# Diagonal sums of five chunks on four 64x64 tiles of TensorE, three unread wide products ahead of it, and every order written anew

## The chip, the cores and the metric

One core of one Trainium2 chip runs the whole program in one launch. The metric is the device time of one execution in microseconds (us); of the kernel before, three executions are shown, and a fourth was profiled.

## What is computed

Four sequences of 768 tokens pass through a recurrent attention with 8 heads of 48 features, and then through a gated network:

```python
for t in range(S):                                   # per batch b and head h
    cur = u * k[t] (outer) v[t]
    y[t] = r[t] @ (state + cur)
    state = w[:, None] * state + k[t] (outer) v[t]   # w, u: one number per head and feature
h = relu(y @ w_in)                                   # 384 -> 1024, halves u and v of 512
v_n = (v - mean) / sqrt(var + 1e-6)                  # over the 512 features
v_s = w_spatial @ v_n + b_spatial                    # over the 768 tokens of the sequence
out = (u * v_s) @ w_out                              # 512 -> 384
```

All of it is float32, and the weights come in float64 halves and other raw forms that the kernel converts itself.

## The kernel before

A sequence is cut into 6 chunks of 128 tokens, so there are 24 chunks, numbered m. The recurrence inside a chunk becomes products: heads are taken in pairs p = 0..3, and a chunk in two halves of 64 tokens, so that a pair's two heads and a chunk's two halves fill the four 64x64 corners of TensorE. For each chunk

- `load` brings r and k with features on partitions (tile rk), and r, k, v with tokens on partitions (rkv);
- `prep` scales rk by powers of the decay (tile tt, a table made at the start from wt: a scan and a reciprocal on VectorE, L346 and L351, then one copy on ScalarE), turns k over on TensorE for the first three chunks ("kt", L434) and makes the diagonal term;
- `scores` makes the products of k and r ("sc", L486) and of k and v ("st", L498) in 64-wide corners;
- `mid` masks the scores into tile a (L509) and moves the state on (sbb L514 or L516, ps L520, sba L526 or L529);
- `xsum` adds state times r ("rs") and scores times v ("av", both L537) in the one accumulator xp;
- `xout` folds xp together (ScalarE copy cp L582, TensorE "xa" L587) and splits the result in a high and a low part xh and xl (L600, TensorE "xl" L604, L606).

xp is a single buffer, so the rs of a chunk begins only when the copies of the chunk before have read it.

The diagonal term is a sum over 48 features of r, k, and a column of weights wu = w times u. For the first five chunks (ND_PE) TensorE makes it ("ds", L450): the product of r and k stands in tile a with two heads on the 128 partitions, and one matmul per pair with a moving operand of two columns (one per head, zero on the other head's partitions) gives two sums per token. For later chunks VectorE reduces instead. The sums go to tile dg, and from there `dia` (L470 on GpSimd, or eight small ScalarE operations) writes them on the diagonal of a.

The network's weights are split in two fp32r parts at the start: w_in in six blocks ("conv": four VectorE steps L634, L636, L639, L646, a ScalarE cast, and three matmuls 128x512 L654 to L656 on TensorE), w_spatial and w_out in a similar way. Every big product is then three fp32r matmuls (`mm3`, L738 to L740): V (nine matmuls 128x512 for a chunk), U, the spatial products, and the output.

The order is not found at run time. A planner in the file (class `Plan`) gave every operation a start, an engine and a buffer; the numbers are kept in the table SCHEDULE, and `plan.replay` reads them. Operations are issued in the order of their starts, so each engine and SyncE's queue of DMA transfers has a fixed order, and only semaphores decide when each begins. The buffers of the w_in conversions and of many products are the four PSUM tiles pm.

Of the kernel before, what the change touches and what calls it, by code (L numbers as in the profile page):

```python
# [11 lines left out]
ALU = mybir.AluOpType  # L12
# [6 lines left out]
P = 128  # L19
# [258 lines left out]
def fused_kernel(ctx, tc, rkT, rkvN, wT, uB, w_in, w_sp, b_sp, w_out, out):  # L278
# [4 lines left out]
    PAD0, PAD1 = 0, 32  # L283
# [38 lines left out]
    def dma(fn, nbytes, r=(), w=(), bufs=()):  # L322
        return op(SPQ, fn, r, w, bufs, nbytes)
# [11 lines left out]
    dma(lambda: nc.sync.dma_start(out=wt, in_=wT), 6144, w=["wt"])  # L335
# [9 lines left out]
    for p in range(NP):  # L345
# [9 lines left out]
    op(("POOL", 0.21, True), lambda: g.tensor_tensor(  # L355
        out=wu.rearrange("s (p j) -> s p j", j=2), in0=wt[:, 0:NP].unsqueeze(2).to_broadcast([P, NP, 2]),
        in1=wt[:, NP:3 * NP].rearrange("s (p j) -> s p j", j=2), op=ALU.mult), r=["wt"], w=["wu"])
# [14 lines left out]
    head = []  # L372
    tp = buf("pm")
# [30 lines left out]
    def prep(m):  # L404
# [24 lines left out]
        else:  # L429
# [5 lines left out]
            t["kt"] = op(("PE", 0.86, False), f, r=[(m, "k"), "eye"], w=[(m, "kt")], bufs=[rk, kp])  # L435
# [3 lines left out]
        if m < ND_PE:  # L439
            at = 448 + H * (m % 2)  # L440
# [13 lines left out]
            o.fn = lambda o=o: (s.copy if o.eng == "ACT" else lambda x, y: v.tensor_copy(out=x, in_=y))(  # L454
                dgs[dg.place].rearrange("s j p -> s p j"), ps[:, 0, at:at + H].rearrange("s (p j) -> s p j", j=2))
# [653 lines left out]
    "00000000h0dr10t08c09307l09u0ar0av0al07l0860b90qv0dc0rr1130qb0fw0qp0zn1431ac08r0c30a000b01902i0500b908r03r069"  # L1109
    "07i0ve0dn1by1870a00z50xw0u516y15r17o19l1gd1dn1ip1n00v50x20yz18713u1a51eq0jk0lh0ne0ol0pb10c1bq1bq1p11sh28x2h1"  # L1110
    "2kr3452372542d72772kv2wc30z1ue2f42iy2l02ms2qj2vd33u0fq0hn0ht0n90jq0u50wf0xw0mp0p011x0r90u61050sg14s0na0s90vv"
    "0yt0uc0y919x1ai16y1dw1ir1fv1o11wb17i18n1de1fb1i31tv2252qo3b41mg1oi11r1gu1gb1vr1ix1qc1x321b21o20929b2282b82c8"
    "1qw1s21uf1zl20t25s2it2q42x123q2d81nn1m41qy1xq2bu2op2tr2fu2hj2xu2p52q52r52ge2im2mr2pv2r832l3in3m73rv3xl3yn43l"
    "48r4au4bd4oj4ky4eo1oi1r02ua30f24827e2xg2fu2oh3ap3ba3a238n3gc3am3bl3fd33538139d3bf3f23kn41u47a47u25s2fu3gr3it"
    "2jf2s835h37n3iv3nk3sq3x43vp41b3xo3l73md3nq3v13w93yh4534cs4if2wc3kn44j46l3lo3ze41545o4454d24fs48f4a44pa4g64lp"
    "4mp4ad4bw4dc4fv4h34kv4r54vo4yl51v53253l54454n55657s5a15ca1pr2hf2mz4bd4lb28a2sk2wa3p25u00wn1ku1ux1jg1s33533y5"
    "4sv3qg4em2713dn4nq2tz2zv19g2op32e2ao2pt36c3zj4b74n73qp53r3cf3hb4gj56f7a07ul4ql52f6nu6ux6wu71q4tc4wy5ej5h24w8"
    "4zl5gw5je59m5qu5x35z862865950m5m65sg62t75v7d85dy6ba6qr6ve73276q55a5v666s6ci6e86ji7ec7yc8598dt8zg9ha7mk7r89ps"
    "9roa61a9q6fm6si78a7ya8do8fc62a66y9b19np9t79ur1ap3p34rb4uf5vj6gi6s974a4t55935qx5yn6l26sa6w97gt2iy3713dt3s4478"
    "48x6tl7at2k731f33y3i93v93wz7k87rd96y9lb9mt8r88xk92588q8f28jnavrb5admkb1vbsvemcaenavwaxe3it32l4xp4ys4ib3f24ow"  # L1120
    "3pp49a4br4ux4wm5cm5bn5jq5nq5165295535a346l48f5ia5kc55p4ve5oh5fj5zm66e60x5zi6fm6hj6ii6jo5mq5nw5r46375nf50m6jy"
    "6m06yh5d361o6a36e277w72l7167es73575o79t6oe6pk6qx6tu6p35m67io7kq7nz68x6wx6do7447cr7wz7vk8aw7zu86t8ct7vx7x47yg"
    "89c5oo6nu8ei8gk81v71h84v7hz87t8q68jt8ie8uy8kd8iy8qk8rw8tf8kw7mk8x08z296g7zg8t38ml8wv9du9e59cq9lh9iu9wba3s97v"
# [91 lines left out]
```

## Time and profile before

| | |
|---|---|
| three executions | 342.02, 343.79, 345.06 us (median 343.79) |
| profiled execution | 345.35 us, of which 343.2 us are the span from first to last instruction |
| TensorE busy | 329.7 us, 96% of the span |
| VectorE, ScalarE, GpSimd busy | 235.5, 169.5, 142.2 us |
| mean granted TensorE clock | 0.994 |

A row of the time line gives start, duration, engine, line, operation, and in brackets the idle time of the engine before it and what ended that. Matmuls overlap, so a row's duration holds some of the next; the chain of waits gives the part by which each piece moved the end on. "x8" counts instructions: a float32 matmul is two, a turn-over (transpose) is one.

### The profile page before, as it was taken

What the parts mean: (1) busy time and instruction counts of PE and PEld (TensorE: products, weight loads), DVE (VectorE), ACT (ScalarE), POOL (GpSimd) and SP (SyncE); (2) the same over time, 40 slices, a digit from 0 to 9 for tenths busy, and PEclk for the clock granted to TensorE, in tenths of its full rate; (3) what the DMA queues carried; (4) which work ended last, traced back from release to release, by engine and by line L of the source; (5) the groups of instructions that cost most, each with busy time, mean ns of one, the idle gap of its engine ahead of it and who ended that gap; (6) DMA issues with size and microseconds to landing.
All of it is one profiled execution on the core that took longest, in us unless ns stands there. A gap on an engine that the chain in (4) does not pass through costs nothing.

```text
span 343.2 us, 13056 instructions
## 1 busy us (share of the span) xinstructions
PE 329.7 (96%) x5832; PEld 301.0 (88%) x5832; DVE 235.5 (69%) x430; ACT 169.5 (49%) x428; POOL 142.2 (41%) x125
## 2 busy tenths in 40 slices
PE   3898999999999999999999999999999999999995
PEld 2767768899999888999999999999999999999995
DVE  6683887987969977769966858477865932726440
ACT  2252456885154365676544626673233776622231
POOL 3637358725829825383834122220944010125100
PEclk9998999999999999999999999999999999999999
DMA  7966676442341558322430440554200001100012
GB/s 233 356 217 238 233 224 247 155 178 97 127 138 43 187 165 270 136 77 85 138 136 5 156 159 3 159 161 150 78 4 2 4 0 70 48 1 2 1 68 92
DMA packets 14455, 41.53 MB, mean 121 GB/s; under 512 B 1728, under 2 KB 5312, under 8 KB 14400
## 3 DMA queue, kind: packets, MB, share of 16 engines
q1 hardware_dynamic: 14400, 40.71, 34.6%
q8 instruction: 45, 0.74, 0.9%
q14 instruction: 10, 0.08, 0.1%
HBM read 35.99 MB, written 4.72 MB: 119 GB/s over the span
## 4 chain that ended last, share of the span: by engine, by line
PE 92%; DVE 3%; DMA 2%; ACT 1%; issue 1%; SPq 0%; ACTq 0%
PE pm L738 25%; PE pm L740 23%; PE pm L739 23%; PE xp L537 9%; PE ps L486 4%; PE ps L498 3%; PE ps L450 2%; DMA raw<-w_in 2%; PE pm L654 1%; PE xp L587 1%; PE pm L434 0%; DVE hb L636 0%; DVE B L700 0%; DVE a L509 0%; DVE pm L634 0%
## 5 line engine op out<-in xcount | busy, mean ns | idle before, releaser
L738 PE MATMUL pm<-B,vh 128*128 128x384 f32 x102 | 34.9, 342 | 0.0
L834 POOL TENSOR_TENSOR g<-g,slot 128x384 f32<-128x384 f32 x14 | 16.2, 1160 | 43.6 <-DVE g L829 37.2
L740 PE MATMUL pm<-B,vl 128*128 128x384 f32 x102 | 34.2, 335 | 0.0
L739 PE MATMUL pm<-B,vh 128*128 128x384 f32 x102 | 34.1, 335 | 0.0
L738 PE MATMUL pm<-xh,wi_h 128*128 128x384 f32 x96 | 32.9, 342 | 0.0
L738 PE MATMUL pm<-wo_h,gt 128*128 128x384 f32 x96 | 32.6, 339 | 0.0
L739 PE MATMUL pm<-wo_l,gt 128*128 128x384 f32 x96 | 32.1, 335 | 0.3 <-issue 0.3
L740 PE MATMUL pm<-xh,wi_l 128*128 128x384 f32 x96 | 32.2, 336 | 0.0
L740 PE MATMUL pm<-wo_h,gt 128*128 128x384 f32 x96 | 32.2, 336 | 0.0
L739 PE MATMUL pm<-xl,wi_h 128*128 128x384 f32 x96 | 32.2, 335 | 0.0
L738 PE MATMUL pm<-wi_h,xh 128*128 128x512 f32 x72 | 29.8, 414 | 0.0
L740 PE MATMUL pm<-wi_h,xl 128*128 128x512 f32 x72 | 28.9, 401 | 0.0
L739 PE MATMUL pm<-wi_l,xh 128*128 128x512 f32 x72 | 28.8, 400 | 0.0
L836 DVE TENSOR_TENSOR gt<-g,gt 128x384 fp32r<-128x384 f32 x32 | 19.7, 622 | 13.1 <-ACT gt L835 13.1
L470 POOL TENSOR_TENSOR a<-diag,dg 128x512 f32<-128x512 f32 x20 | 23.2, 1162 | 13.3 <-ACT dg L454 7.6
L812 ACT ACTIVATE slot<-pm 128x384 f32<-128x384 f32 x32 | 15.6, 493 | 23.8 <-PE pm L740 23.8
L835 ACT CAST gt<-g 128x384 fp32r<-128x384 f32 x32 | 16.1, 508 | 19.1 <-POOL g L834 8.4
L738 PE MATMUL pm<-T,vh 128*128 128x384 f32 x72 | 24.4, 339 | 0.0
L582 ACT COPY cp<-xp 128x256 f32<-128x256 f32 (+1 forms) x24 | 8.5, 353 | 32.1 <-PE xp L537 27.0
L766 ACT ACTIVATE vs<-pm 128x512 f32<-128x512 f32 x24 | 14.4, 600 | 20.1 <-PE pm L740 20.1
L848 POOL TENSOR_TENSOR vl<-vs,vh 128x768 fp32r<-128x768 f32 x6 | 12.2, 2027 | 29.1 <-ACT vh L846 19.2
L740 PE MATMUL pm<-T,vl 128*128 128x384 f32 x72 | 24.1, 335 | 0.0
(148 smaller groups left out, 927.5 us busy)
## 6 DMA issues: line engine op xcount, KB each, us to landing
rkv<-rkvN SPq DMA_DIRECT2D x19, 608.0 KB, 4.9
rk<-rkT SPq DMA_DIRECT2D x21, 512.0 KB, 4.9
slot<-w_sp SPq DMA_DIRECT2D x12, 384.0 KB, 5.8
out<-ob SPq DMA_DIRECT2D x24, 192.0 KB, 2.4
raw<-w_in SPq DMA_DIRECT2D x6, 512.0 KB, 7.4
rk<-rkT SPq DMA_DIRECT2D x6, 256.0 KB, 5.4
rawo<-w_out SPq DMA_DIRECT2D x4, 384.0 KB, 5.9
rkv<-rkvN SPq DMA_DIRECT2D x2, 416.0 KB, 4.0
```

The lines of the kernel that those rows point to most:

```text
L470: g.tensor_tensor(out=A, in0=diag.unsqueeze(1).to_broadcast([P, H, HC]), in1=G.unsqueeze(2).to_broadcast([P, H, HC]), op=ALU.mult)
L486: te.matmul(ps[s0:s0 + 64, j, p * HC:(p + 1) * HC], R[hd, 1, p, s0:s0 + 64], R[hd, 0, p, t0:t0 + 64], start=True, stop=True, skip_group_ch ...
L537: te.matmul(xp[32 * p:32 * p + 32, bank, BASE[bank, z] + jt * HC:BASE[bank, z] + (jt + 1) * HC], lhsT, rhs, start=(bank, p) not in began, ...
L738: te.matmul(o, lh, rh, start=first, stop=False, skip_group_check=skip)
L739: te.matmul(o, lh, rl, start=False, stop=False, skip_group_check=skip)
L740: te.matmul(o, ll, rh, start=False, stop=last, skip_group_check=skip)
L766: op(("ACT", 0.79, False), lambda: s.activation(out=V, in_=pms[pm.place], func=AF.Relu, accum_out=su), r=[(b, "vp", c)], w=K + [("mv", n, ...
L812: op(act(TH, True), lambda: s.activation(out=slot(ub_, d % 2), in_=pms[pm.place][:, 0:TH], func=AF.Relu, scale=2.0), r=[(b, "up", t, d)], ...
L834: o.fn = lambda o=o: pick(o.eng).tensor_tensor(out=slot(gb), in0=slot(gb), in1=slot(ub_, d % 2), op=ALU.mult)
L835: op(act(TH), lambda: s.copy(slot(gt, 0), slot(gb)), r=[k], w=[(b, "gh", t, d)], bufs=[gt, gb], near=near)
L836: op(dve(TH, True), lambda: v.tensor_tensor(out=slot(gt, 1), in0=slot(gb), in1=slot(gt, 0).bitcast(F32), op=ALU.subtract), r=[k, (b, "gh", ...
L848: o.fn = lambda o=o: pick(o.eng).tensor_tensor(out=lv(), in0=src(), in1=hv().bitcast(F32), op=ALU.subtract)
```

## The change

- The ds of the first five chunks is cut into corners: 16 matmuls per chunk, each 64 partitions by 64 tokens with a moving operand of one column, in place of 4 of 128 by 128 with two columns. wu has one column per pair in place of two, wt shrinks from 12 to 8 columns, and the sums lie in both banks of ps.
- Three float32 matmuls of the identity with itself, 512 columns wide, are written into three pm tiles ahead of the first real TensorE work. Nobody reads them. They need only the tile eye (the identity, made on GpSimd).
- SCHEDULE is replaced whole: starts, engines and buffers of all operations. `pad0` changes from 0 to 8, a tile that nothing reads.

```diff
-    wt, w128, wu = T("wt", [3 * NP]), T("w128", [NP]), T("wu", [2 * NP])
+    wt, w128, wu = T("wt", [2 * NP]), T("w128", [NP]), T("wu", [NP])
...
+    def warm(b):
+        te.matmul(pms[b.place], eye, eye.unsqueeze(1).to_broadcast([P, 4, P]), start=True, stop=True)
+    for n in range(3):
+        wb = buf("pm")
+        head.append(op(("PE", 0.92, False), lambda wb=wb: warm(wb), r=["eye"], w=[("warm", n)], bufs=[wb]))
...
-            t["kt"] = op(("PE", 0.86, False), f, r=[(m, "k"), "eye"], w=[(m, "kt")], bufs=[rk, kp])
+            t["kt"] = op(("PE", 0.60, False), f, r=[(m, "k"), "eye"], w=[(m, "kt")], bufs=[rk, kp])
...
-            at = 448 + H * (m % 2)
+            at = 448 + NP * (m % 2)
...
-                    te.matmul(ps[:, 0, at + 2 * p:at + 2 * p + 2], PR()[:, p], wu[:, 2 * p:2 * p + 2],
-                              start=True, stop=True, skip_group_check=True)
-            t["ds"] = op(("PE", 0.50, False), f2, r=[(m, "a"), "wu"], w=[("psD", m % 2)], bufs=[a])
+                    for j in range(2):
+                        for z, s0, t0 in SUBS:
+                            hd = slice(64 * j, 64 * j + 64)
+                            te.matmul(ps[s0:s0 + 64, j, at + p:at + p + 1], PR()[hd, p, s0 // 64], wu[hd, p:p + 1],
+                                      start=True, stop=True, skip_group_check=True)
+            t["ds"] = op(("PE", 0.45, False), f2, r=[(m, "a"), "wu"], w=[("psD", m % 2)], bufs=[a], tiled=True)
...
 SCHEDULE = (
-    "00000000h0dr10t08c09307l09u0ar0av0al07l0860b90qv0dc0rr1130qb0fw0qp0zn1431ac08r0c30a000b01902i0500b908r03r069"
+    "02i00000h02x2950df0e60ex0fo0gl0gf0xr0df0370510u700005v0v30hp0b50fk0610lg0m50mu0x115m01o00f03s00b00005007i08r"
...
```

What the table does to the order is shown at three places; the numbers behind a tile's name tell its buffers apart, and new lines stand 4 to 7 further down in the file. The first is TensorE's beginning. Before:

```order
L375 MATMUL pm_115<-eye,tt 128x128
L434 MATMUL pm_116<-eye,rk_99 128x128 x4
L486 MATMUL ps<-rk_99 64x64 x16
L498 MATMUL ps<-rkv_102 48x48 x16
L375 MATMUL pm_115<-eye,tt 128x128
L537 MATMUL xp<-rk_99,sbb 32x64 x16
L450 MATMUL ps<-wu,a_94 128x2 x4
L434 MATMUL pm_116<-eye,rk_100 128x128 x4
L450 MATMUL ps<-wu,a_95 128x2 x4
L375 MATMUL pm_115<-eye,tt 128x128
L654 MATMUL pm_117<-hb,eye 128x512
L655 MATMUL pm_117<-lw,neg 128x512
```

With the change:

```order
L373 MATMUL pm_115<-eye 128x512
L373 MATMUL pm_116<-eye 128x512
L373 MATMUL pm_117<-eye 128x512
L379 MATMUL pm_118<-eye,tt 128x128 x3
L438 MATMUL pm_115<-eye,rk_99 128x128 x4
L493 MATMUL ps<-rk_99 64x64 x16
L505 MATMUL ps<-rkv_102 48x48 x16
L438 MATMUL pm_117<-eye,rk_100 128x128 x4
L457 MATMUL ps<-wu,a_94 64x1 x16
L544 MATMUL xp<-rk_99,sbb 32x64 x16
L379 MATMUL pm_118<-eye,tt 128x128
L661 MATMUL pm_116<-hb,eye 128x512
```

The second ds (of chunk 1) has moved from before the first w_in conversion to behind the second one, and behind the third conversion come now the scores and the k-v products of chunk 2 ahead of the first V; before, these two stood behind it.

The second place is SyncE's queue at the start. Before:

```order
L335 DMA wt<-wT 128x12
L395 DMA rk_99<-rkT 128x512 x2
L619 DMA raw<-w_in 128x1024
L401 DMA rkv_102<-rkvN 128x448
L395 DMA rk_100<-rkT 128x512 x2
L619 DMA raw<-w_in 128x1024
```

With the change:

```order
L399 DMA rk_99<-rkT 128x512
L399 DMA rk_100<-rkT 128x512
L335 DMA wt<-wT 128x8
L399 DMA rk_100<-rkT 128x512
L399 DMA rk_99<-rkT 128x512
L626 DMA raw<-w_in 128x1024
```

The small transfer wt, from which the table tt is made, stands third, behind two transfers of 256 KB.

The third place is VectorE from the end of the table tt to the last step of the first w_in conversion (lw). Before:

```order
L351 RECIPROCAL tt<-tmp 128x4x64
L416 TENSOR_TENSOR rk_99<-rk_99,tt 128x512
L418 TENSOR_TENSOR rk_99<-rk_99,tt 128x512
L634 TENSOR_SCALAR pm_117<-raw 128x512
L636 SCALAR_TENSOR_TENSOR hb<-raw,pm_117 128x512
L639 TENSOR_SCALAR pm_117<-hb 128x512
L646 SCALAR_TENSOR_TENSOR lw<-raw,pm_117 128x512
```

With the change:

```order
L351 RECIPROCAL tt<-tmp 128x4x64
L420 TENSOR_TENSOR rk_99<-rk_99,tt 128x512
L422 TENSOR_TENSOR rk_99<-rk_99,tt 128x512
L420 TENSOR_TENSOR rk_100<-rk_100,tt 128x512
L641 TENSOR_SCALAR pm_116<-raw 128x512
L521 COPY sbb<-ps 128x4x48
L643 SCALAR_TENSOR_TENSOR hb<-raw,pm_116 128x512
L646 TENSOR_SCALAR pm_116<-hb 128x512
L353 TENSOR_TENSOR w_72<-tmp 128x4
L422 TENSOR_TENSOR rk_100<-rk_100,tt 128x512
L527 TENSOR_TENSOR ps<-sbb,ps 128x192
L653 SCALAR_TENSOR_TENSOR lw<-raw,pm_116 128x512
```

Five rows that stood behind the first conversion, or elsewhere, now stand inside it or ahead of it.

## Rows read from the trace of the kernel before

**Rows 1.** Busy time of the engines by stretch: stretch, its length, busy us (instructions), clock, DMA.
```profile
43.00:60.00 17.00, 16.14 (x386) 12.48 (x387) 13.57 (x25) 10.21 (x29) 11.47 (x11) 1.00 0.69 236
60.00:100.00 40.00, 40.00 (x885) 37.34 (x880) 34.32 (x69) 23.28 (x58) 21.60 (x17) 1.00 0.40 136
...
200.00:300.00 100.00, 99.74 (x1628) 93.61 (x1616) 65.03 (x126) 53.89 (x127) 27.11 (x20) 1.00 0.21 72
```

**Rows 2.** The chain that ended last, in order of time, opening: start, us, what.
```profile
7.45 0.71 DVE pm L634
...
11.32 1.80 PE ps L450 x8
...
16.02 1.71 PE pm L654 x2
...
18.64 0.79 PE xp L537 x53
19.43 0.62 PE ps L486 x32
20.05 0.42 PE xp L587 x2
20.47 0.86 PE pm L654 x2
...
21.80 0.51 PE ps L498 x32
22.31 0.40 PE xp L604 x2
22.71 0.44 PE pm L434 x4
```

**Rows 3.** The same chain from the third conversion to the last ds.
```profile
25.40 1.37 issue
...
27.51 0.98 PE ps L450 x8
28.50 0.88 PE xp L587 x4
29.37 0.43 PE pm L738
...
32.24 0.23 PE pm L739
...
37.53 1.02 PE ps L450 x8
...
42.37 0.80 PE ps L450 x8
```

**Rows 4.** Busy time by stretch again, around the clock's fall.
```profile
25.40:29.00 3.60, 2.23 (x64) 2.14 (x63) 3.03 (x6) 0.37 (x1) 3.60 (x4) 0.94 1.02 409
28.50:31.90 3.40, 3.40 (x11) 2.82 (x12) 0.36 (x1) 0.94 (x3) 2.91 (x4) 0.51 0.66 257
```

**Rows 5.** DMA issues of the first 3 us: count, KB each, us from issue to landing.
```profile
rk<-rkT SPq DMA_DIRECT2D x2, 256.0 KB, 2.9
...
wt<-wT SPq DMA_DIRECT2D x1, 6.0 KB, 1.7
```

**Rows 6.** Time line, SyncE's queue: the first two transfers of rk.
```profile
1.24 0.89 SPq L395 DMA_DIRECT2D rk<-rkT  x2
```

**Rows 7.** Time line of TensorE, its first row.
```profile
5.49 0.45 PE L375 MATMUL pm<-eye,tt 128*128 128x128 f32 x1 [5.49 <-DVE tt L351]
```

**Rows 8.** Time line of VectorE, opening.
```profile
3.60 1.74 DVE L351 RECIPROCAL tt<-tmp 128x256 f32<-128x256 f32 x1
5.54 0.69 DVE L416 TENSOR_TENSOR rk<-rk,tt 128x512 f32<-128x512 f32 x1 [0.20 <-DVE tt L351]
...
13.15 0.36 DVE L520 TENSOR_TENSOR ps<-sbb,ps 128x192 f32<-128x192 f32 x1 [1.92 <-PE ps L450]
...
16.77 0.73 DVE L509 COPY_PREDICATED a<-mask,ps 128x512 f32<-128x512 uint32 x1 [1.20 <-ACT sba L529]
```

More of the change, by code (lines that the diff above doesn't have):

```diff
@@ L334, in fused_kernel @@
     tb = buf("slot", "tmp")
-    dma(lambda: nc.sync.dma_start(out=wt, in_=wT), 6144, w=["wt"])
+    dma(lambda: nc.sync.dma_start(out=wt, in_=wT), 4096, w=["wt"])
     def q_(): return slot(tb)[:, 0:256].rearrange("p (n c) -> p n c", n=NP)
@@ L354, in fused_kernel @@
        r=QS, w=["w128"], bufs=[tb])
-    op(("POOL", 0.21, True), lambda: g.tensor_tensor(
-        out=wu.rearrange("s (p j) -> s p j", j=2), in0=wt[:, 0:NP].unsqueeze(2).to_broadcast([P, NP, 2]),
-        in1=wt[:, NP:3 * NP].rearrange("s (p j) -> s p j", j=2), op=ALU.mult), r=["wt"], w=["wu"])
+    op(("POOL", 0.21, True), lambda: g.tensor_tensor(out=wu, in0=wt[:, 0:NP], in1=wt[:, NP:2 * NP], op=ALU.mult), r=["wt"], w=["wu"])
     op(("POOL", 0.21, False), lambda: g.memset(eye, 0.0), w=["eye"])
@@ L1114 @@
[L1114 to L1123, printed above, removed]
@@ new lines @@
+    "0p40y10sc1c21ew1kk1mp1n91a11dk1ro1fd1gc1ta1de1en1gp1jw1l42932fd2ko2qm1mm1wt1bc1i31r220j1q625f29m2bm1yz2702hr"
+    "28n2m22n81zj23a25z28329n2gv2ue33g35t2et2qn17r1xe2kj2ej2st2yy2zy2xm2ue3852w12ze3762td2vh2y630k3243cx3lj3sz3tj"
+    "3w23yt41t42c4dz4iu4oo4kw4qx1r22st3913b322s2a333r2st2zb34039l3l23jn3mz3lm3rz3zc3dh3eo3g63iz3k73vk4cq4ig56d2gv"
+    "1yz3ms3p22we3gu2i32p32lo3ow3vp43d41y46r45s3ry3w33zd41a42i44q4g94j053u3e63qw4as4cu3ym43v4764cf4a04ei4mt4eo4gd"
+    "4xv4sq51g53z4f84gf4jk4m44nc4r44xe53a58w5bf5du5fv5is5jb5ju5p15kj5ms1ba1rw4sc4bb4dl12121v26c1qh4ur21h3qk3s434f"
@@ new lines @@
+    "36s1ds3p558r2ja32h2u25gp5rg3wm4j822q3nq5nh2wl3na4h65tn5435fd4ms51y3qw3y14hg5db80x85t4wu5bz7av7wk73r7gz4zl5b6"
+    "5ra5tv4t651262265k5kj5ys64069w6fg6je5fv63g68c6b16e16ng58r6dv6vm6xc72h75v5ov6zf74b7707a07u07l98598a58f08kh8mv"
+    "7w99259qy9ti9wia9g6i76ur78y85b9cp9ff6976mj9gy9mza0za7x2083c44ln50g5kd6dv7ib7sg55c5wj6qk6t36u37cn7fn7x31sb2o4"
+    "2qn42v60061q6wc79u2i43663d43fu3ir3kg4vj7kw96h9u2aad9oza55b4t89l8j58rhbb0bulf0ybl4cj1d19atwb7ic4p4fx3cx516529"
+    "55r3qg4ge3uk3xa43u5d35es5qk5gf5xi5yo5eo5hf5ie5p03ou4eo5t75v94pc4wb5dg4y152f5g95x367s6cz6kx6s36z35xn5yu6gu6lx"
@@ new lines @@
+    "5zl5436qv6sx6zr5lx6ga5om6bf6i678379s7ai7eg7ov7pv6vb6x67bf7cx6x95x37pl7rn7hw6hu7nc6kj77e7jn7th7v68bp8dm8el8fr"
+    "7vk82l8758fl6w06ur8l38n58hf7qx89a81183r8c38oz8qo8wg8sb8pj8v98wm91g8q88ap9c99eb99z8qq8tq8zw96w9e39g59hu9v19sh"
+    "9wyafk9lk9mr9qj9th8rr8yd95g9ml7fj7r48o39xw8fd8lw8on98ra4la5ba5uab0abjac2axlat3avc9ix9rva0faiy9ura2ea6haaia0h"
+    "a71a98ad1alhb0eb2xb8obbqbexbfmblgbhv5yc6e86p072s7oh7fh80x82i7xx7zh7zb86g6xo7vk89g8jy8kg8yd9gk9129ba9k59p49qp"
+    "9419j097c9pe9toa46a6daeuakhbxbazub3bbnpcowc0ac73b19c9wa94bk4adsam1ai4arr8xt960b6cbbkbgsbt9ap8b2ndp2ducbqcc4t"
@@ new lines @@
+    "mg9miyn2hnkimyhn3dmu5n4xnbhngdn75nc1nk5np1nwuo3do4ynftnm2nqqntqnvbo1ho6io81ohtojensto9lob5okkomhok9oplor4osu"
+    "oueofxokyoo1ow9oxuoudp0pp27oa5oghohzoolouxowfp05p31p4hp6hp7zp8tpbppd5pf5pgnp5xpelpg1pi1pjj"
+    " "
+    "000000000000000000000000000000000000000000000000000000000000000000000000000000000000000000000000100100000100"
+    "000010000000010000000000010001010000001000000000001011010000000000000000000000000000010010000000000000000000"
+    "000100100000000000000000000100100000000000000000000000000000101001000010100100001010000100000000000000000000"
@@ new lines @@
+    "000000000000000000000000000000000000000000000000000010100000100100000010000100000000000010000100001000010000"
+    "100001000000000000000000000000000100000000000000000100000000000000000001110000000100000000001000000000000000"
+    "000101000000000000000000000000000000000000000000000000000000000000000000000000000010000000001010010000001000"
+    "000000000000001000000000000000000000000000000000000000000000000000"
+    " "
+    "01203001012300213226101411011309023a211c30002110000000131101100011302110220111335427530b83600d13a235019c7042"
@@ L1192 @@
     wt[:, :D] = w.reshape(NP, 2, D).transpose(1, 2, 0)
-    ut = np.zeros((2, 64, NP, 2), u.dtype)
-    for j in range(2):
-        ut[j, :D, :, j] = u.reshape(NP, 2, D)[:, j].T
+    ut = np.zeros((2, 64, NP), u.dtype)
+    ut[:, :D] = u.reshape(NP, 2, D).transpose(1, 2, 0)
     rows = [h * D + d for h, d in features()]
```

73 lines of the change are left out of this document (29 added, 44 removed).

## The prediction

> **What bounds the kernel now.** I read first how busy each engine is by stretch, then the chain of waits, then the time lines of the opening. The stretches [rows 1] show TensorE filled from 60 us on: 40.00 of 40, and still 99.74 of 100 from 200 us on. From there the end is a fixed amount of TensorE work away, and nothing that VectorE, ScalarE or the transfers do shows. Only in the first 60 us can TensorE be early or late, and work taken off it anywhere counts in full.
>
> In the opening the reader is to see three things. The first matmul waits 5.49 us for the table tt [rows 7], which follows wt through the scan and the 1.74 us reciprocal [rows 8]. [...] Third, the clock falls again: over 28.50 to 31.90 us the granted clock is 0.51 [rows 4], and one matmul of the first V takes 0.43 in place of 0.23 us [rows 3]. Ahead of that fall stand 1.37 us in which TensorE waited for nothing that the profile shows ("issue") and 0.98 us of the two-column ds [rows 3]: TensorE was busy 2.23 of 3.60 us [rows 4].
>
> **The sum.** I follow TensorE to its first V (29.37 us now [rows 3]) and then count what it still has to do.
>
> *The three wide products.* [...] The first real step that matters (kt) also waits for a VectorE scaling of 0.69 us, so I take 0.
>
> *wt third in the queue.* Two issues take 0.89 us [rows 6], so it is issued 0.9 us later. If it also waits for the second 256 KB transfer, issued 0.45 us after the place that wt has now and landing 2.9 us after that [rows 5], where wt took 1.7, it lands 0.45 + 2.9 - 1.7 = 1.7 us later. Between 0.9 and 1.7 I take 1.5, near the upper end, since all of them stand in one queue. Then tt is ready at 3.60 + 1.74 + 1.5 = 6.8 us.
>
> *To the first conversion.* VectorE then does three scalings of rk at about 0.65, four conversion steps at 0.71, a copy of 0.35, a small product of 0.2, another scaling and the state sum of 0.36 [rows 2, 8]; the copy, like the state sum, has 192 columns, and the small product is an estimate below that: 1.95 + 2.84 + 0.35 + 0.2 + 0.65 + 0.36 = 6.4, so lw is there at 13.2 and TensorE begins the conversion at 13.3 us. Now it begins at 16.02 [rows 2]: there TensorE was late itself, with two ds of 1.80 us each ahead of it.
>
> *From there to the first V.* At the higher level the rows give [rows 2]: three conversions at 0.86 + 2 x 0.23 = 1.32 (3.96; the two last matmuls of one have the width of those of V, 0.23 [rows 3]), two av at 0.79, two sc at 0.62, two st at 0.51, xa 0.42 and, with twice the columns, 0.84, two xl at 0.40, one kt 0.44, rs at the 0.62 of sc, and two ds. A tiled ds was never run; its bounds are 0.36 (less than the st above, which has corners of 48) and 0.98, what it costs now [rows 3]. The sc has the same 16 corners, with 64 columns in place of one, and takes 0.62, so I take 0.5. That makes 3.96 + 1.58 + 1.24 + 1.02 + 1.26 + 0.80 + 0.44 + 0.62 + 1.0 = 11.9 us. Waits: VectorE has eight conversion steps, a masking of 0.73 [rows 8], two state sums and a scaling between the first lw and the third, 7.8 us, against 7 us of TensorE work, so 0.8; for ScalarE's copies between two groups on xp I allow 0.9. V begins at 13.3 + 11.9 + 1.7 = 26.9 us. Gain: 2.5.
>
> *What is left then.* One sc and one st are done that now come behind the first V: 1.1. Two later ds, now 1.02 and 0.80 [rows 3], become 0.5: 0.8. The cold stretch cost six matmuls of V 0.20 us each (0.43 against 0.23 [rows 3]) and a seventh 0.1: 1.3, if it does not come again. With everything kept: 2.5 + 1.1 + 0.8 + 1.3 = 5.7.
>
> *What I take off.* The three products are dense, but what follows is not: from 6.8 to 13.3 us TensorE has two kt, one sc, one st, one ds, one rs and four turn-overs, some 3.5 us of small pieces with waits between, as in the stretch ahead of the fall [rows 3, 4]. So I expect a cold stretch between 9 and 30 us, at the 1.3 us of the one seen. The 1.37 us of "issue" came in a stretch of many small matmuls with the DMA engines full (1.02 [rows 4]); the new order has such a stretch too and 24 more matmul instructions per ds, so I expect it again: 1.4. The fall after it and the rest of the opening's waits (TensorE idle 0.9 of the 17 us from 43 to 60 [rows 1]) I leave at what they cost, but for 0.6 us: VectorE is busy 13.57 us there, and a TensorE that comes earlier finds it less far on. 5.7 - 1.3 - 1.4 - 0.6 = 2.4.
>
> Against its own execution that is 345.35 - 2.4 = 342.95 us; that execution lies 1.56 above the median of 343.79, so for the median I say **341.4**.
>
> [...]
>
> **The rivals.**
> 1. *The clock holds and the issue wait does not come back.* For it: the conversions, which are wide, begin 2.7 us earlier. Against: the sparse stretch above. 5.7 - 0.6 = 5.1 stay: 340.25 in the profiled execution, 338.7 for the median.
> 2. *VectorE takes it back later.* If TensorE reaches the 43 to 60 us stretch 4 us early and VectorE, with 13.57 of 17 us busy [rows 1] and the same work, is the one that ends last there, nearly all goes: 0.3 left, median 343.5. Against: the share is not full.
> 3. *Slower: the warm start dies at once.* If the clock falls in the sparse stretch before 13.3 us and stays low until V, the conversions cost 3 x 1.3 more (double), two ds 2 x 0.4, and kt, rs, two sc, two st, two xa and two xl 0.3 each on average, an estimate between nothing and double: 7.7 in all. About 1.7 hides in the waits that I counted, so V comes at 32.9, 3.5 later than now; 1.9 of the terms behind V and the 1.3 of the present fall go against it, and the issue wait adds 1.4. That gives 343.79 + 3.5 - 1.9 - 1.3 + 1.4 = 345.5; with wt at its upper bound and the same 0.6 given back, 346.3. It is slower than now once more than about 6 us of this cold price are paid.
> 4. *The tiles bring nothing.* If sixteen one-column corners take the 0.93 of four wide ones, the two later ds lose 0.8 and two of those before V 0.9: 343.1. The sc row speaks against it.
>
> **How the numbers follow.** I give my sum 0.45, the rivals 0.20, 0.15, 0.14 and 0.06. Within 1% (3.4 us, about what a measurement of this kernel can tell) means 340.4 to 347.2. My sum's own range is 339.5 to 343.2, by the bounds of wt (0.6 less, 0.2 more), the ds (four at 0.14 less or 0.4 more) and the waits that I allowed (0.9); a fifth of it is over 1% faster. With the first rival that makes 0.30 faster; a third of the third rival with 0.05 for an unseen new wait in the later order makes 0.10 slower; 0.60 stays. The range 338.0 to 345.6 leaves out the far ends of rivals 1 and 3.
>
> **What would show it.** Right: the three L373 rows end by 7.5 us; the turn-over behind them waits for tt at 6.5 to 7.5 us; the first L661 starts near 13.3 us, released by VectorE's lw; the first V starts between 26 and 28.5 us; a ds of 32 instructions takes 0.4 to 0.6 us; a clock of 0.5 is seen once more before 30 us. Wrong: wt landing over 1.7 us later than now; conversions at 1.71 us a pair throughout; TensorE idle for more than 1.5 us between 30 and 60 us, which would be rival 2; or idle beyond 60 us, which I have no row for.

## The result, and the profile after

The changed kernel takes **347.31 us** (median of 12 runs, 343.82 to 348.86), the kernel before 344.22 on the same chip (12 runs): a ratio of 1.0082, 95% interval 1.0052 to 1.0111. It is 3 us slower; the forecast was 2.4 us faster. The profiled execution took 348.48 us, its span 346.5. All ratios here leave out executions over 1.5% above the fastest of their kernel; medians take all.

The stretches of [rows 1] read as follows after the change (columns as there):

```profile
43.00:60.00 17.00, 14.00 (x390) 11.29 (x386) 11.22 (x26) 8.96 (x25) 10.78 (x10) 0.90 0.46 164
60.00:100.00 40.00, 40.00 (x883) 36.67 (x882) 30.22 (x56) 26.14 (x69) 24.03 (x20) 1.00 0.34 119
200.00:300.00 100.00, 99.72 (x1686) 93.73 (x1685) 66.62 (x129) 53.43 (x130) 23.03 (x17) 1.00 0.22 71
```

From 60 us on TensorE is as full as it was, and at 60 us it has 3.3 us more busy time left than the kernel before had then, so the whole loss lies in the first 60. In 43 to 60 TensorE is idle 3.0 of 17 us; it was 0.9. Who made it wait, over the whole span:

```profile
PE xp L544 <- issue: 2.5, 1, 2.5
PE pm L373 <- POOL eye L357: 2.3, 1, 2.3
PE ps L493 <- issue: 1.9, 1, 1.9
PE pm L661 <- DVE lw L653: 1.5, 1, 1.5
PE ps L505 <- DMA rkv<-rkvN: 1.2, 1, 1.2
```

and the time line of the opening and of the two "issue" waits (start, duration, and in brackets the idle time ahead):

```profile
2.29 5.49 PE L373 MATMUL pm<-eye 128*128 128x512 f32 x6 [2.29 <-POOL eye L357]
7.57 0.64 PE L379 MATMUL pm<-eye,tt 128*128 128x128 f32 x3
10.64 0.58 PE L505 MATMUL ps<-rkv 64*48 64x48 f32 x32 [1.17 <-DMA rkv<-rkvN]
11.84 0.64 PE L457 MATMUL ps<-wu,a 64*64 64x1 f32 x32
14.60 2.03 PE L661 MATMUL pm<-hb,eye 128*128 128x512 f32 x2 [1.47 <-DVE lw L653]
...
25.66 0.57 PE L493 MATMUL ps<-rk 64*64 64x64 f32 x22
28.13 0.44 PE L493 MATMUL ps<-rk 64*64 64x64 f32 x10 [1.91 <-issue]
...
50.96 0.58 PE L505 MATMUL ps<-rkv 64*48 64x48 f32 x32
51.35 0.66 PE L493 MATMUL ps<-rk 64*64 64x64 f32 x32
51.94 0.45 PE L544 MATMUL xp<-rk,sba 64*32 64x64 f32 x32
52.51 0.45 PE L544 MATMUL xp<-rk,sbb 64*32 64x64 f32 x31
55.46 0.24 PE L544 MATMUL xp<-rk,sbb 64*32 64x64 f32 x1 [2.50 <-issue]
```

Both waits split a run of like instructions (22 | 10, 31 | 1) whose operands were there, as the pieces ahead ran with them. After each, and at the first conversion, the granted clock is 0.51 to 0.52 (TensorE alone: stretch, length, busy, granted clock, DMA share, GB/s):

```profile
14.60:17.90 3.30, 3.30 (x39) 0.51 1.03 403
28.10:35.10 7.00, 6.97 (x88) 0.52 0.74 290
55.50:59.00 3.50, 3.50 (x73) 0.52 0.60 213
```

**What "issue" is here.** The queue "q8 instruction" on the page carries 46 transfers for 2 x 5958 TensorE instructions (matmuls and weight loads): 0.75 MB / 46 = 16 KB, and one transfer for some 259 of them. Before it was 45 for 2 x 5832.

```profile
PE 332.7 (96%) x5958; PEld 301.2 (87%) x5958; DVE 235.6 (68%) x424; ACT 175.5 (51%) x451; POOL 145.3 (42%) x127
q8 instruction: 46, 0.75, 0.9%
```

Counted in the trace, with TensorE's semaphore instructions among them (33 before, 38 after), the issue waits of both kernels come ahead of an instruction 449 + 256 n: 705 before, 961 and 2241 after, and one of 0.3 us beyond 200 us in each (9665, 9409). By these counts the instructions reach TensorE in blocks of 256, and with the place 193 each of the two kernels has as many such borders as transfers (45 and 46). In the two traces the transfer of a block starts, ahead of these five waits, after the border before it has been passed: 0.8 us after it at the two waits of 0.3, with the DMA engines idle until it starts, and 4.6, 3.2 and 2.4 us after it at those of 1.37, 1.91 and 2.50, where loads filled 77, 92 and 96% of the DMA engines in between. (Among wide products, where nothing waits, it also started up to 3.4 us before that instruction ran.) It takes 0.9 to 1.3 us at these five, and TensorE goes on 1.3 to 1.6 us after it has landed. Around the second wait, the transfers from 50.60 to 53.00 us and from 53.00 to 54.10 show it:

```profile
DMA packets 230, 0.90 MB, mean 375 GB/s; under 512 B 25, under 2 KB 25, under 8 KB 230
q1 hardware_dynamic: 230, 0.90, 93.8%
```
```profile
DMA packets 9, 0.02 MB, mean 19 GB/s; under 512 B 7, under 2 KB 7, under 8 KB 8
q8 instruction: 1, 0.02, 5.5%
q1 hardware_dynamic: 8, 0.00, 1.3%
```

A border was passed at 50.67. Until 53.0 an rk and an rkv load (1.1 MB) fill the engines (93.8%); only then comes the block, with next to nothing beside it (1.3%). The 256 short instructions between began within 2.08 us; TensorE ran dry at 52.96 and went on at 55.46.

### The profile page after: what moved, and what is told of

Same layout as the page of the kernel before. It is cut to its first block, busy times and chain, and to the rows that moved or that the text cites. A ratio compares the mean times of both kernels' runs of the same rounds, so it can differ in the third digit from the quotient of the medians.

```text
span 346.5 us, 13330 instructions
## 1 busy us (share of the span) xinstructions
PE 332.7 (96%) x5958; PEld 301.2 (87%) x5958; DVE 235.6 (68%) x424; ACT 175.5 (51%) x451; POOL 145.3 (42%) x127
## 4 chain that ended last, share of the span: by engine, by line
PE 93%; DMA 2%; issue 2%; DVE 1%; POOL 1%; SPq 1%; ACT 0%; ACTq 0%; DVEq 0%
PE pm L745 25%; PE pm L746 23%; PE pm L747 23%; PE xp L544 10%; PE ps L493 4%; PE ps L505 3%; DMA rkv<-rkvN 2%; PE pm L661 2%; PE ps L457 1%; PE xp L611 1%; SPq L399 0%; PE pm L663 0%; PE pm L662 0%; PE xp L594 0%; POOL a L448 0%
## 5 line engine op out<-in xcount | busy, mean ns | idle before, releaser
L477 POOL TENSOR_TENSOR a<-diag,dg 128x512 f32<-128x512 f32 x19 | 22.2, 1173 | 44.9 <-DVE dg L466 42.5
L843 DVE TENSOR_TENSOR gt<-g,gt 128x384 fp32r<-128x384 f32 x32 | 21.3, 672 | 18.9 <-ACT gt L842 18.9
L745 PE MATMUL pm<-xh,wi_h 128*128 128x384 f32 x96 | 33.6, 350 | 0.0
L841 POOL TENSOR_TENSOR g<-g,slot 128x384 f32<-128x384 f32 x10 | 11.8, 1179 | 46.7 <-DVE g L836 46.7
L424 DVE TENSOR_TENSOR rk<-rk,tt 128x1024 f32<-128x1024 f32 x17 | 23.7, 1393 | 2.6 <-DMA rk<-rkT 2.6
L745 PE MATMUL pm<-T,vh 128*128 128x384 f32 x72 | 24.5, 340 | 0.0
L746 PE MATMUL pm<-T,vh 128*128 128x384 f32 x72 | 24.1, 335 | 0.0
```

Of the source, the lines that this page charges most:

```text
L424: op(dve(1024, True), lambda: v.tensor_tensor(out=rks[rk.place], in0=rks[rk.place], in1=tt.unsqueeze(1).to_broadcast([P, 2, NP, C]), op=AL ...
L477: g.tensor_tensor(out=A, in0=diag.unsqueeze(1).to_broadcast([P, H, HC]), in1=G.unsqueeze(2).to_broadcast([P, H, HC]), op=ALU.mult)
L745: te.matmul(o, lh, rh, start=first, stop=False, skip_group_check=skip)
L746: te.matmul(o, lh, rl, start=False, stop=False, skip_group_check=skip)
L841: o.fn = lambda o=o: pick(o.eng).tensor_tensor(out=slot(gb), in0=slot(gb), in1=slot(ub_, d % 2), op=ALU.mult)
L843: op(dve(TH, True), lambda: v.tensor_tensor(out=slot(gt, 1), in0=slot(gb), in1=slot(gt, 0).bitcast(F32), op=ALU.subtract), r=[k, (b, "gh", ...
```

## The experiments

Theory 1: the loss is waits for instruction blocks, which come where 256 short instructions run off faster than the next block arrives, and the cold stretches after them. Theory 2: the new order is too crowded as it is, and the waits go with that. "Issue" counts waits of 0.2 us and more in the profiled execution. Beyond 60 us both kernels have one of 0.3, and most variants one near 225 us; these are listed from 1 us on. Ratios are to the kernel before, run in turn on the same chip, and tell more than the medians: the kernel before has medians from 343.34 to 345.36 us in the groups of runs here.

| run | median us (runs) | ratio, 95% interval | issue waits up to 60 us |
|---|---|---|---|
| after | 347.31 (12) | 1.0052 to 1.0111 | 1.9, 2.5 |
| fill84 | 362.61 (4) | 1.0409 to 1.0582 | 1.1, 0.75; eleven more beyond 60, 14.0 in all |
| noprod | 348.13 (4) | 1.0039 to 1.0199 | 2.6, 1.8 |
| wide_new | 348.78 (4) | 1.0055 to 1.0207 | 1.1; 1.6 at 225 |
| tiles_old | 349.98 (10) | 1.0063 to 1.0144 | 4.4, 0.85 |
| order_only | 350.32 (4) | 1.0083 to 1.0209 | 1.6, 2.8; 1.0 at 227 |
| rk_early | 346.52 (10) | 0.9990 to 1.0072 | 1.6, 1.9 |
| loads_both | 347.49 (10) | 1.0028 to 1.0106 | 1.95, and 0.5 off a border |
| wt_first | 347.29 (10) | 1.0000 to 1.0078 | 3.5 in three, longest 2.2 |
| three_loads | 345.69 (11) | 0.9977 to 1.0053 | 1.3, 1.9 |
| three_loads_v | 344.74 (11) | 0.9968 to 1.0038 | 0.3, 1.3, 0.3; 1.2 at 224 |
| five_loads | 346.29 (12) | 1.0000 to 1.0075 | 0.7, 1.7 |
| five_loads_st | 346.28 (12) | 0.9996 to 1.0079 | 0.3, 1.6, 1.1 |
| old_loads | 343.60 (10) | 0.9941 to 1.0010 | none |
| old_loads_again | 344.28 (12) | 0.9962 to 1.0023 | 0.3 |
| before_light | 343.24 (11) | 0.9933 to 1.0000 | 0.4 |
| after_light | 344.87 (11) | 1.0013 to 1.0091 | 1.0, 2.5 |
| after_light_wt | 344.60 (11) | 0.9957 to 1.0035 | 2.9 in two |

### Moving the borders: fill84

```diff
 # after: 21 unread corner matmuls of one column (84 instructions) ahead of the first conversion
+                if key == ("in", 0):
+                    filler(21)
                 te.matmul(PM(), eye, HB().bitcast(F32), start=True, stop=False)
```

> The changed kernel with 21 more corner matmuls (64x64, one column, unread) in the idle 1.47 us ahead of the first w_in conversion: 84 more TensorE instructions (42 matmuls, 42 weight loads), nothing else. Theory 1, instruction supply: TensorE's instructions come in 16 KB transfers on a DMA queue of their own (46 in the changed kernel for some 11,950 instructions), and it stops where it has used up a block before the next has landed; what counts is where the block's border falls. 84 further on, the border at 52.96 us comes at about 48 us, among wide products, so the 2.50 us wait is gone and the low clock behind it (about 1 us): 343.5 to 344.5 us; the wait of 1.91 at 26 us may stay or move by a little. Theory 2, crowding: the waits belong to the moments at which the DMA engines are full, whatever the instruction: both waits stay at 26 and 53 us, and the time is 347.3 to 348.

Neither came out: 362.61 us. The wait at 53 did go, as theory 1 had it (a border now falls at 54.3 and costs nothing), but moving all later borders by 84 put them into the short products that every chunk brings, and TensorE stood still for 14.0 us beyond 60 us (profiled execution, 368.53 us), where each of the two kernels had lost 0.3. One of eleven waits, with the pieces around it:

```profile
111.39 0.69 PE L499 MATMUL ps<-rk 64*64 64x64 f32 x32
111.91 0.27 PE L511 MATMUL ps<-rkv 64*48 64x48 f32 x7
113.59 0.51 PE L511 MATMUL ps<-rkv 64*48 64x48 f32 x25 [1.42 <-issue]
```

84 instructions of one column cost some 15 us by the medians. That is the border's place, not work: the block waits alone are 15.8 us against 4.7. My size failed for looking only at the first 60 us. The change itself adds 252 matmuls and weight loads (257 instructions with the semaphore instructions), nearly one block, so its later borders lie close to where they lay; that it lost nothing beyond 60 us was luck of that number.

### Parts of the change: noprod, wide_new, tiles_old, order_only

```diff
 # noprod: after without the three products
-        te.matmul(pms[b.place], eye, eye.unsqueeze(1).to_broadcast([P, 4, P]), start=True, stop=True)
+        return
 # wide_new: after with the wide ds, wt and wu of the kernel before
 # tiles_old: before with the tiled ds, wt and wu of the change
 # order_only: after with both, no products and the wide ds
```

> The changed kernel without the three wide products. They are 12 instructions, so the borders move by 12. Theory 1: both waits stay, 1.9 us near 26 and about 2 us near 53; without the products the opening runs at the lower level until about 18 us, but conversion 0 does so in the changed kernel too (2.03 us for its first pair), so kt, sc, st, ds and rs cost 1.5 us more in the stretch from 7.6 to 12.9 us, in which VectorE's lw at 14.6 hides most: 347 to 348 us. Rival, the products carry the opening: 349 or more.

> The changed kernel with the old diagonal sums: four matmuls of two columns a chunk in place of sixteen corners; 48 instructions fewer per sum, 240 in all. Theory 1: the borders move back by 48 at each sum, by 240 at 53 us, so the 2.50 us wait there comes elsewhere or goes (3.5 less with its low clock), and the five sums cost 0.35 to 0.4 each more (1.9): 345 to 346 us. Theory 2: both waits stay at their times and only the sums count: 349.

> The kernel before with the sums on corners alone: its own order, its own opening, no products; 240 instructions more. Theory 1: two sums at the lower clock give 0.8 each where TensorE ends last (11.3 to 16 us), three give 0.4: 2.0 to 2.8 less, and the 1.37 us wait at 25.4 moves, since 96 more instructions stand ahead of it: 340 to 342.5 us, if no new border falls badly. Theory 2: the wait stays at 25.4 us: 341.5 to 342.5. If the corners themselves cost the time: 344 or more.

> The new order alone: without the three products and with the sums as they were, wide. As many TensorE instructions as before, so every border beyond 60 us lies near where it lay. Theory 1: at least one issue wait of over 1 us between 20 and 60 us, where short products follow each other, and 345 to 348. If the new order gains what it was drawn up for and the tiles and products lose it: 341 to 343.

noprod came near what was expected: 348.13, with waits of 2.6 and 1.8. The other three are slower than theory 1 had them, each with its waits at other places, but up to 60 us always at a border of the count. wide_new's time, 348.8, is the one that theory 2 named, but its waits are not at theory 2's places: the one at 53 us is gone. tiles_old's time would also fit corners that cost time by themselves; its trace has 5.2 us of block waits where the kernel before has 1.4. In tiles_old the border falls near 23.6 us by the count, ahead of 128 short matmuls, the tiled ds among them, with the DMA engines full (the share of the loads is 101.2% from 23.7 to 27.2 us); the worst wait of all follows:

```profile
24.08 0.82 PE L538 MATMUL xp<-a,rkv 64*32 64x64 f32 x62
24.84 0.63 PE L451 MATMUL ps<-wu,a 64*64 64x1 f32 x29
29.86 0.37 PE L451 MATMUL ps<-wu,a 64*64 64x1 f32 x3 [4.39 <-issue]
```

The order alone is the slowest (1.0146): two waits of 1.6 and 2.8 us. The medians of the parts taken out (order_only 350.3, wide_new 348.8, noprod 348.1, after 347.3) would give the products and the tiles some gain within the new order, of the size of the intervals. The loss is the order's.

### The same instructions, other loads: rk_early, loads_both, wt_first

The starts in the table set the order of issue, so one number moves one transfer. 239 is chunk 5's rk load, 289 a w_sp load, 394 a w_out load, 0 wt. TensorE's instructions stay as they are.

```diff
-            o.start = int(starts[3 * o.n:3 * o.n + 3], 36) / 100
+            o.start = {239: 43.52}.get(o.n, ...)                            # rk_early
+            o.start = {239: 43.52, 289: 26.91, 394: 26.92}.get(o.n, ...)    # loads_both
+            o.start = {0: -0.01}.get(o.n, ...)                              # wt_first
```

> The changed kernel with one load issue moved: chunk 5's rk load (SyncE, 49.03 in its trace) is issued ahead of the rkv load that waits for TensorE until 48.6. TensorE's instructions are the same, in the same order. Theory 1 (TensorE waits for its own instructions, and their 16 KB transfer stands behind 1.1 MB of loads at 49.5 to 53.0): the transfer starts some 1.6 us earlier, the issue wait of 2.50 us at 52.96 falls to 0.8 to 1.4, and the time to 345.0 to 346.5. Theory 2 (the wait belongs to the short instructions themselves, whatever the DMA does): the wait stays at 2.5 and the time at 347 to 348.

> The same, and two more loads moved back: the w_sp slot of 19.84 and the w_out load of 23.48 behind the two w_sp loads of 27.0. TensorE's instructions are the same. Theory 1: the wait of 1.91 us at 26.23 falls to 0.3 to 1.2 as well, and the time is 343.5 to 345.5. Theory 2: both waits stay, 347 to 348; or later, if the moved loads are missed where they are used.

> The changed kernel with wt first in SyncE's queue instead of third. If the late wt is what TensorE pays for at the start, the transposes of the factors begin near 5.5 us instead of 7.57, the first rows of V come 1 to 2 us earlier, and the time is 345.3 to 346.5. If the waits behind them (the rkv load at 10.64, the lw half at 14.60) end where they end now, only the opening moves and the time stays at 347 to 348. By theory 1 both issue waits stay, at whatever instruction falls on the border then.

rk_early: the short products ahead of the wait run 1.3 us earlier (L493 at 50.08 in place of 51.35), and the wait is 1.91 in place of 2.50, between the two theories; the rkv load was not moved. The time lies at the upper end of theory 1's. loads_both took the wait at 26 away, which theory 2 does not allow. But VectorE then waited 1.72 us for the w_out load that I had moved, TensorE 2.1 us for VectorE's copy of the state (sbb) behind it, and the time stayed at 347.49, theory 2's. wt_first's median stayed at 347.29, but its ratio is 1.0039 where the change has 1.0082: some 1.5 us, with intervals that overlap. The trace does not show this as the price of a late wt. TensorE's turn-overs of tt start at 7.49 in place of 7.57, with the three products just ahead of them, and the first conversion starts no earlier, since it waits for VectorE's lw as before:

```profile
14.71 2.07 PE L661 MATMUL pm<-hb,eye 128*128 128x512 f32 x2 [1.48 <-DVE lw L653]
```

What did change is the wait near 26 us, 0.59 in place of 1.91, with no low clock seen behind it (1.00 from 30 to 45 us, and the ds at 28.04 is a row of 0.64).

### Several loads together: three_loads, three_loads_v, five_loads, five_loads_st

```diff
+            o.start = {0: -0.01, 239: 43.52, 289: 26.91}.get(o.n, ...)      # three_loads
+            # three_loads_v: and 176: 47.00, 177: 47.41 (the nine products of V behind L611, L505, L493)
+            # five_loads: three_loads and 284: 32.45, 299: 32.46 (two more w_sp loads)
+            # five_loads_st: five_loads and 201: 43.525 (L505 ahead of V)
```

> The changed kernel with three load issues moved: wt first in SyncE's queue, chunk 5's rk ahead of the rkv load of 48.6, and the w_sp load of 19.84 behind those of 27.0 (the w_out load of 23.48, missed by VectorE when it was moved too, stays). TensorE's instructions are the same. Theory 1: the issue wait near 26 falls from 1.91 us to 0 to 0.8, the one near 50 to 1.6 to 2.2, and the time is 342.5 to 345, below the kernel before or level with it. If what makes the changed kernel slow is its order and not the waits for instructions: 346 to 348.

> The same three loads, and one piece of TensorE's order: the nine wide products of V that run at 48.50 in the changed kernel's trace go behind L611 and the sums L505 and L493, so that they stand between two groups of short products that now run without a break. The instructions are the same in number. Theory 1: the 256 instructions ahead of the border then take some 4 us instead of 2.1, and the second issue wait falls to 0 to 0.8 as well: 341.5 to 344. Theory 2 (crowding by itself): no less than three_loads has.

> three_loads with two more loads moved: the two w_sp loads of 27.0 go behind the rk and w_out loads of 36.5, since in three_loads the instruction transfer of 27.6 to 32.5 stood behind them and TensorE waited 1.5 us at 32.4. Theory 1: that wait goes (0 to 0.4), the one near 51 stays at 1.6 to 2.2, and the time is 0.8 to 1.8 us below three_loads: 343.5 to 345, a ratio of 0.995 to 0.999. If the waits for instructions are no longer what holds the new order back: no change, 1.000 to 1.003, with other waits in their place.

> five_loads, and the sum L505 of the chunk goes ahead of the nine wide products of V (at 48.5 in the changed kernel's trace) instead of behind them, which puts the wide products into the 256 instructions ahead of the border without the wait for ScalarE that three_loads_v got by moving V. Theory 1: no issue wait of over 0.6 us is left between 20 and 60, and the time is 341.5 to 344, a ratio of 0.990 to 0.997: below both kernels. If the waits are not all: 0.998 to 1.003.

three_loads and three_loads_v came to 1.0015 and 1.0003 of the kernel before: moving three transfers, and one piece of TensorE's order, brings the changed kernel level. Neither gained all that theory 1 gave it: 345.69 lies between the two theories, 344.74 just above the 344 of theory 1, and a new wait of 1.3 us came at the next border, near 33 us. In three_loads_v the interval (0.9968 to 1.0038) no longer meets that of the change itself. The wait near 51 fell from 1.9 to 0.3 with the wide products between the short ones, and 1.4 us for ScalarE's xh came up in its place, as did a block wait of 1.2 at 224 us (0.3 in the change):

```profile
PE xp L544 <- issue: 1.6, 2, 1.3
PE ps L505 <- DMA rkv<-rkvN: 1.6, 1, 1.6
PE pm L661 <- DVE lw L653: 1.5, 1, 1.5
PE xp L611 <- ACT xh L607: 1.4, 1, 1.4
PE pm L746 <- issue: 1.2, 1, 1.2
```

The five loads were a miss: waits near 32 and 50 us stayed, and the time went back to 1.004. Their runs spread from 342.5 to 349.4 us; one profile of such a kernel is not its median.

### The wait of the kernel before: old_loads, old_loads_again

```diff
+            o.start = {296: 22.24, 375: 22.25}.get(o.n, ...)    # before: a w_sp and a w_out load behind rk
```

> The kernel before with two loads moved back: the w_sp slot of 20.34 and the w_out load of 20.82 behind the rk and w_sp loads of 25.3. TensorE's instructions are the same. Theory 1: the issue wait of 1.37 us at 25.40 falls to 0 to 0.5, the low clock after it goes with it, and the time is 342.0 to 343.5. Theory 2: the wait stays and the time is 344 to 345.

> The kernel before with two loads moved back, as in old_loads, in more rounds. If taking away the one issue wait is worth what it measured there: 0.995 to 0.9985 of the kernel before. If that was chance: 0.999 to 1.002.

TensorE now passes the place of [rows 3] without a stop; the pieces that were split there (11 | 51) are whole:

```profile
24.89 0.25 PE L537 MATMUL xp<-rk,sbb 64*32 64x64 f32 x3
24.95 0.83 PE L537 MATMUL xp<-a,rkv 64*32 64x64 f32 x62
25.70 1.05 PE L450 MATMUL ps<-wu,a 128*128 128x2 f32 x8
```

The granted clock from 26 to 36 us is 1.00, where it was 0.82 up to 30 us and 0.83 behind. In old_loads_again a wait of 0.33 stayed. So the mechanism holds for the old wait too. Its worth is less sure: 0.9976 and 0.9993, both intervals with 1 in them, at most 2 us and likely under 1, where my prediction's prices (1.4 and 1.3) would make 2.7.

### The loads cut away: before_light, after_light, after_light_wt

```diff
-        dma(lambda: nc.sync.dma_start(out=slot(rb), in_=w_sp[j * P:(j + 1) * P, :]), 393216, w=[("raws", j)], bufs=[rb])
+        dma(lambda: nc.sync.dma_start(out=slot(rb)[:, 0:64], in_=w_sp[j * P:(j + 1) * P, 0:64]), 393216, w=[("raws", j)], bufs=[rb])
 # and the four w_out loads in the same way; the readers take one column over and over
```

> The kernel before with the six w_sp and four w_out loads of the first 90 us cut to a twelfth of their size or less (their readers read one column over and over, so what is computed with these weights is left out): 3.5 MB less for the DMA engines, TensorE's instructions the same. Theory 1: no issue wait of over 0.4 us is left before 60 us, and the time is 342.0 to 344.0.

> The changed kernel with the same loads cut in the same way. Theory 1 (the miss is waits for instructions behind loads): the wait of 1.91 us at 26 falls to 0 to 0.6, the one of 2.50 near 53 (behind an rk and an rkv load, which stay) to 1.2 to 2.5, and the time is 342.5 to 345.0, within 1.5 us of before_light. Rival (the new order loses elsewhere too): 2.5 us or more above before_light.

> after_light with wt first in SyncE's queue. Theory 1: another 0.5 to 1.5 us off after_light, 341.0 to 344.0, level with before_light or below. Rival: 345 or more.

These kernels leave most of the two weights out, and only their times count. before_light came as expected, but for a wait of 0.44. after_light is 1.6 us above it by the medians, just over theory 1's bound of 1.5, and 0.9% above it by the ratios, which is the rival's side: no decision. What is left in after_light is two waits for blocks; the second is the one behind the rk and rkv loads, which stayed:

```profile
PE xp L544 <- issue: 3.5, 2, 2.5
PE pm L373 <- POOL eye L357: 2.3, 1, 2.3
PE ps L505 <- DMA rkv<-rkvN: 1.6, 1, 1.6
```

wt first takes the ratio from 1.0052 to 0.9996, some 1.9 us, but the median only from 344.87 to 344.60. With wt_first that is the same direction twice, each time with intervals that overlap; that a late wt costs is not shown.

**What stands.** Theory 2 falls as far as the waits go: with the same TensorE instructions they went, came and changed length with the loads, and moving three loads took the changed kernel from 1.0082 to 1.0015. That step also moves wt, and its interval (0.9977 to 1.0053) just touches the change's; with three_loads_v it is clear of it.

How much of the loss is the waits and how much the lower clock is not separated. The 12 executions of the change go with their mean granted clock: the three with the highest (0.988 to 0.995) took 343.8 to 344.8 us, about what the kernel before takes, the three with the lowest (0.975 to 0.979) 348.5 to 348.9. The new order loses without it too: order_only's profiled execution, at a mean clock of 1.000 and with waits of 1.6, 2.8 and 1.0 us, took 347.0, above all 29 executions of the kernel before on that chip. That the waits bring the clock down is not shown; two of the three falls begin at one, but not every wait has a fall behind it. **Open** is also whether the new order would beat the old one with no wait left. No kernel here got there, and none beats both: old_loads is the nearest, with 1 in its interval.

## Why the prediction was wrong

**The step that failed** is the one on the 1.37 us of "issue". I took it for a property of a stretch of many small matmuls with the DMA engines full, expected it once, and put 1.4. Those are the conditions, but the place is set by a count: in both kernels it comes at an instruction 449 + 256 n at which the next block is late. The change moved and thickened the short products, and two borders fell into such runs: 1.91 and 2.50 us, 3.0 more than the 1.4. The term next to it failed by more: one cold stretch at 1.3 us. There were three, and by the ledger below they cost some 4.7 more than that. I also counted "24 more matmul instructions per ds" as a risk at one place, and not that five sums and the three products move every border behind them.

The ledger, by my own terms, against the profiled execution (342.95 forecast, 348.48 measured, 5.5 apart):

- *First V at 26.9, measured 32.07 on the chain: 5.2 late.* The first conversion began at 14.60 in place of 13.3 (1.3). wt landed 2.0 us later than before, not 1.5 (VectorE's scan starts at 4.60, and 1.7 was my upper bound), but by wt_first that did not decide. VectorE waited 0.70 for the w_in load and 0.62 for TensorE's sums behind an rkv load, which the chain shows; I had nothing for either. The first conversion then ran cold, 14.60 to 17.49 on the chain, 2.89 in place of 1.32 (1.6). The issue wait took 1.91. The products that the wait split and the pieces from there to V, at 0.52 of the clock but for the first, cost 4.5 in place of 2.9 (1.6: 0.55 + 0.44 + 1.15 + 0.96 + 0.72 + 0.67 against 0.62 + 0.84 + 0.5 + 0.51 + 0.40). Of the 1.7 of waits that I allowed almost nothing came. 1.3 + 1.6 + 1.9 + 1.6 - 1.7 = 4.7; 0.5 stays unassigned. Since I had the issue wait's 1.4 apart, the net is 3.8. The rows, of the chain and of VectorE:

```profile
3.58 6.92 DMA rkv<-rkvN
...
32.07 0.48 PE pm L745
```
```profile
10.02 0.69 DVE L641 TENSOR_SCALAR pm<-raw 128x512 uint32<-128x512 uint32 x1 [0.70 <-DMA raw<-w_in]
11.34 0.36 DVE L521 COPY sbb<-ps 128x192 f32<-128x192 f32 x1 [0.62 <-PE ps L505]
```

- *The second issue wait*, 2.50, for which I had nothing in the sum, only a chance of 0.05, and its cold stretch: nine products of U at 0.32 and more in place of 0.17, 1.2, and 0.3 on the one ahead of them. Together 4.0.
- *Given back*: between 30 and 60 us the kernel before waited for VectorE and ScalarE, 1.2 us in three rows of its time line; the change has one wait of 0.38 for GpSimd there:

```profile
37.53 1.02 PE L450 MATMUL ps<-wu,a 128*128 128x2 f32 x8 [0.36 <-DVE ps L520]
47.47 0.86 PE L537 MATMUL xp<-a,rkv 64*32 64x64 f32 x64 [0.35 <-DVE a L509]
54.09 0.46 PE L537 MATMUL xp<-rk,sba 64*32 64x64 f32 x32 [0.51 <-ACT xl L606]
```

  I had left these as they were and charged 0.6 more: 1.4 better. 3.8 + 4.0 - 1.4 = 6.4, against 5.5; 0.9 is not assigned.

Of these the lower clock makes about 1.6 + 1.6 + 1.5 = 4.7, beside the 1.3 at the first V that was in the sum.

**What was right.** The products end near 7.6 us, just past the 7.5 that I had named. No run shows the 0 that the sum takes for them as a term of its own; what the runs show is that tt's turn-overs begin at 7.57, right behind the products, that kt begins at 8.17 behind VectorE's scaling of rk, and that without the products (noprod) the time was 348.13, not less. The tiled ds is a row of 0.64, and 0.57 on the chain where the clock is high (0.5 taken); at a clock of 0.52 it is 0.96, near the 0.98 of the wide one at 0.94 [rows 3, 4]. The first V's cold matmuls cost the 1.3 that I put. One column saves next to nothing over 64 here: the ds row of 0.64 stands beside 0.69 for the scores. Beyond 60 us nothing shows but the 0.3 that both kernels have. One cold stretch between 9 and 30 us was in the sum; there were two, and a third at 55.5. Of the signs of being wrong, wt over 1.7 us later and the idle between 30 and 60 us came.

Two slips in the working change nothing: the second of the two ds ahead of the old first conversion took 1.63 on the chain, not 1.80, and the bounds named for my sum reach down to 339.3, not 339.5.

**The rivals.** Rival 3 named the right side and a near time (345.5 to 346.3), but not the mechanism: the clock did fall with the first conversion (0.51 from 14.60 to 17.90), was up again at 19.88 (a pair in 0.86), and fell again, to 0.52 up to 35, only after the wait. Rival 2's sign, idle of over 1.5 us between 30 and 60, did show, but the DMA queue made it, not VectorE, which is busy 11.22 us from 43 to 60, less than before. Rival 4 is out by the ds row. My chance of 0.10 for slower was too low mostly because I gave an unseen wait a chance of 0.05 when the trace of before already had one such wait without a cause.

## What to carry to other kernels

An "issue" wait that splits a run of like instructions is worth counting out. Here, up to 60 us, in both kernels and in the variants that had them, the waits of over 0.6 us stood at such places, a multiple of 256 of TensorE's instructions from each other. So TensorE waited for its own program, and the edits that added or removed instructions ahead (84 in fill84, 240 in tiles_old) put other instructions on those places. Count the engine's semaphore instructions too (33 and 38 here). It hurt most where the 256 ran off fast, small matmuls with their weight loads, and loads filled the DMA engines: in some 1.8 us (23.65 to 25.47) ahead of the 4.4 of tiles_old and in 2.1 us ahead of the 2.50 of the change, but in 3.2 us ahead of each of the waits of 0.3. Wide products among them shortened the wait (1.9 to 0.3 us in three_loads_v), and moving large loads away from the few us ahead shortened it or took it away (1.37 to none in old_loads and 0.3 in old_loads_again). Few loads alone did not do it: fill84 waited 1.9 us at 269 us, in a stretch (from 200 us on) with a mean DMA share of 0.15. A reorder is then priced by where the borders fall, not only by the work that it moves.

## What the runs showed of the hardware

- In both kernels TensorE's instructions come in transfers of 16 KB, one for 256 of them (46 in the change, 45 before), on a queue of their own, and start later where loads fill the DMA engines: 2.4 to 4.6 us after the border before, against 0.8 with idle engines. At each of the two waits of 0.3 us the start (0.8), the transfer (1.1 and 1.3) and the restart (1.6 and 1.3) add up to 3.4 us, and the 256 instructions ahead had run off in 3.2.
- A border cost from nothing to 4.4 us: 4.4 at one of tiles_old; in the change 1.9, 2.5 and 0.3 us at three of its 46, and under 0.2 us of TensorE's time at each of the others.
- A wait of 1.9 to 2.5 us was followed by 3.5 to 7 us at the lower clock in the change (0.52); in after_light one of 2.5 us was not (clock 1.00 from 50 to 60 us; stretch, length, TensorE's busy time, clock, DMA share, GB/s).

```profile
50.00:60.00 10.00, 7.41 (x203) 1.00 0.45 159
```
